# Shares of attention transposed by VectorE and ScalarE in place of TensorE, from group 10 on

## Chip, core and metric

The kernel runs on one core of one Trainium2 chip. The metric is the device time of one execution in microseconds. The engines go by the names of the profile: PE is TensorE, DVE is VectorE, ACT is ScalarE, POOL is GpSimd, SP issues the DMAs. Each engine works through its own queue of instructions in order.

## What is computed

Windowed attention over 8 batches of 8 heads, 576 positions and 64 columns a head, in fp32, and behind it a channel-mixing block with a one-step time shift. Cut to what matters:

```python
scores = scale * np.matmul(q, k.transpose(0, 1, 3, 2))
mask = (rel >= 0) & (rel < 64)                 # rel = query position - key position
attn = softmax(where(mask, scores, -1e9))      # shares
x = np.matmul(attn, v)                         # heads side by side: 8 x 576 x 512

x_prev = x shifted by one position
xk = mu_k * x + (1 - mu_k) * x_prev
xr = mu_r * x + (1 - mu_r) * x_prev
k = np.maximum(xk @ w_k, 0)                    # 512 -> 1024
v = k * k @ w_v                                # 1024 -> 512
r = 1 / (1 + np.exp(-(xr @ w_r)))              # 512 -> 512
out = r * v
```

The weights arrive as 64-bit floats and are turned to fp32 on the chip.

## The kernel before

**Blocks and groups.** The 576 positions of a batch are 9 blocks of 64. Two consecutive blocks of the 72 form a group (36 groups, `GROUPS`). A query block meets at most its own and the previous block of keys, so a group needs 2 x 64 query rows of all heads. A group's scores fill one bank of PSUM, as 128 partitions (two halves of 64 query rows) by 8 pairs of head and block, by 128 keys.

**Attention of a group** (`soften`, line 464). VectorE folds the 128 keys of each row into 64 (`pack`: each row's window takes exactly 64 of them), takes the maximum (`most`), subtracts it (`less`); ScalarE takes the exponential (`exp`); VectorE sums (`total`), inverts the sums (`shares`) and multiplies (`scale`), so that the tile `pr` (128 x 512) holds the shares. In the groups of `LEAN` the subtraction, the exponential and the sum are eight ScalarE instructions instead (`exps`), one for each of the 8 pairs, with the maximum as bias and an accumulated sum. The value products need the shares with the keys on the partitions. That transposition is `flip` (line 516): four TensorE transposes of 128x128 into the PSUM tile `t`. VectorE then writes them to SBUF twice, multiplied by two masks (`keep`, line 521), as the tile `pt`: keys of the own block and keys of the previous block. The value products (`values`, 48 or 64 small matmuls) read `pt` and write the PSUM tile `x`, which ScalarE copies to `xu` (`keep_x`).

**Bursts.** `burst` (line 391) issues the scores of group t and the values of group t-1 together on TensorE; in the first groups they are issued apart.

**Units.** The channel mixing runs over units of 4, 5 and then nine times 7 blocks (448 columns). In each unit the blended inputs `xk` and `xr` are split into a rounded part and a rest (`high` on ScalarE, `low` on VectorE), as are the weights and the squares `ks`, and each product is three matmuls per chunk instead of one in full fp32. Eight `k` products take 12 matmuls each, four `r` products 12, four `v` products 24: 240 matmuls a unit. In the first unit the products are plain fp32. ScalarE empties the banks of k and r (three activations per k product, four per r product), VectorE those of v; the results are stored by SP. Three PSUM banks (`m`) are shared by all products.

**The order of the work** comes from a planner in the program. Each `Piece` (line 103) has an engine, a key, an assumed cost, the pieces it needs and the buffers (`Hold`) that it takes and uses. `play` (line 117) walks through an assumed time: an engine that is free takes the ready piece of lowest key. A piece is ready when each piece it needs on another engine has been done for a `lag` (160 ns if not given otherwise), for TensorE pieces of key 60 or more for another 1500 ns (`SLACK`, `STEADY`), and when its buffers are free. The order found is each engine's order on the chip. The keys of the attention groups stand in `BEGIN` (line 42), those of the decoding of the 28 weight chunks in `DECODE`, of their splitting in `SPLIT`, of the first two units' blends in `MIX_0` and `MIX_1`; unit u has keys from 40 u on. `ORDER` (line 54) is the order in which SP issues the first loads (`w` is the next weight chunk, `k0` the keys of group 0).

Of the kernel before, what the change touches and what calls it, by code (L numbers as in the profile page):

```python
# [10 lines left out]
F32 = mybir.dt.float32  # L11
# [7 lines left out]
P = 128  # L19
# [16 lines left out]
TB = 6  # L36
# [2 lines left out]

STEP = 6  # L40
USTEPS = 40
BEGIN = (-81.5, -50.0, -17.0, -17.0, -3.5, 20.0, 21.0, 55.5, 61.0, 70.0, 70.5, 79.5, 93.5, 113, 123, 133, 143,
    153, 163, 173, 183, 196, 210, 223, 236, 250, 263, 277, 286, 295, 304, 312, 322, 332, 342, 352)
DECODE = (0.0, -63.5, -41.0, -15.5, -38.5, -58.0, -19.5, -38.5, -43.0, -28.5, -43.0, -34.5, 45.5, 53.5, 33.5,
    38.0, 46.0, 75.5, 36.5, 48.0, 11.0, 32.0, 34.5, 61.0, 31.0, 41.0, 79.5, 57.5)
MIX_0 = (-78.0, -17.5, -25.5, 6.0)
MIX_1 = (-59.5, -87.5, 44.5, 59.0)
SPLIT = (36.5, 8.5, 54.5, 56.0, 41.5, 47.0, 58.5, 18.5, 55.5, 155.0, 60.0, 133.0, 98.5, 82.0, 77.0, 111.0,
    104.5, 69.5, 168.0, 137.0, 172.5, 109.5, 143.5, 44.0, 125.0, 94.0, 130.5, -3.5)
PE_LOW = set()  # L50
LEAN = {0, 1, 2, 3, 4, 5, 8, 10, 11}
SPARE = {512: 1, 256: 2}
LOADED = 6
ORDER = (*"w w w k0 v2 w q0 v0 w w v1 k1 q1 w w w w q2 w w v3 w w w w k3 w k2 w v5 w k5 w w k4 w q4".split(),
         *"q3 w w w w q5 v4 w w".split())
LINK = 160
SLACK = 1500
STEADY = 60
# [7 lines left out]
def attn_rwkv_kernel(ctx, tc, qT, kT, v2, mu_k, mu_r, w_k, w_v, w_r, out):  # L66
# [3 lines left out]
    at = ctx.enter_context(tc.tile_pool(name="at", bufs=2))  # L70
    act = ctx.enter_context(tc.tile_pool(name="act", bufs=1))
    tmp = ctx.enter_context(tc.tile_pool(name="tmp", bufs=2))
# [5 lines left out]
    class Engine:  # L78
# [5 lines left out]
        def __getattr__(self, name):  # L84
# [1 line left out]
            return lambda *args, **kw: tc.keep_in_program_order(op(*args, **kw))  # L86

    pe, dve, sca, pool, dma = (Engine(e) for e in (nc.tensor, nc.vector, nc.scalar, nc.gpsimd, nc.sync))
    room = {"tmp": TB, "m": 3, "s": 1, "t": 1, "x": 1, "pr": 2, "sums": 4, "pt": 2, "xu": 2,
            **{f"w{wc}": count for wc, count in SPARE.items()}, "ks": 8, "r": R_BUFS, "xr": 1, "xk": 1, "q": 2, "k": 2, "v": 3}  # L90

    def slow(key):
        return SLACK if key >= STEADY else 0
# [103 lines left out]
    for j in range(2):  # L197
        rows = slice(j * W, (j + 1) * W)
# [43 lines left out]
    def decode(n, loaded):  # L242
        ws, _, i, c, wc = chunks[n]
        key = DECODE[n]
        word = Hold("tmp")
# [27 lines left out]
    def split(n):  # L273

        ws, _, i, c, wc = chunks[n]
        key = SPLIT[n]
        ps, bank = [], Hold("m")
# [80 lines left out]
    def block(g, s):  # L358
        return divmod(2 * g + s, NB)

    banks, weights, sums, flipped, sided, crossed = {}, {}, {}, {}, {}, {}
    xs_of, got, opened_x = {}, {}, {}
    chain = {}

# [26 lines left out]
    def burst(key, gs, gv):  # L391
# [31 lines left out]
        if gs is not None:  # L423
            soften(key, gs, p, takes[0])
# [36 lines left out]
    def wide(tile_, count):  # L461
        return tile_.unsqueeze(1).to_broadcast([P, count, W])

    def soften(key, g, p, bank):
        rows, sm = Hold("pr"), Hold("sums")

        lean = g in LEAN
        both = block(g, 0)[1] and block(g, 1)[1]

        def pack():  # L470
            s4 = banks[g]
            weights[g] = at.tile([P, 8, W], F32, name="pr", bufs=2)
            sums[g] = [at.tile([P, 8], F32, name=nm, bufs=4) for nm in ("most", "sums", "rs")]
            if both:
                s8 = s4.rearrange("q h e k -> q (h e) k")
                dve.copy_predicated(s8[:, :, :W], wide(own.bitcast(U32), 8), s8[:, :, W:])
                return
            for s in range(2):
                for h in range(2):
                    e = s4[:, h, 2 * s:2 * s + 2]  # L480
                    if block(g, s)[1]:
                        dve.copy_predicated(e[:, :, :W], wide(own.bitcast(U32), 2), e[:, :, W:])
                    else:
                        dve.tensor_add(e[:, :, :W], e[:, :, W:], wide(hide, 2))

        def most():
            s8 = banks[g].rearrange("q h e k -> q (h e) k")
            dve.tensor_reduce(sums[g][0], s8[:, :, :W], axis=AX.X, op=ALU.max)
            if lean:
                dve.tensor_scalar_mul(sums[g][0], sums[g][0], -SCALE)  # L490

        def less():
            s8 = banks[g].rearrange("q h e k -> q (h e) k")
            dve.tensor_sub(weights[g], s8[:, :, :W], sums[g][0].unsqueeze(2).to_broadcast([P, 8, W]))

        def exp():
            sca.activation(weights[g], weights[g], AF.Exp, scale=SCALE)

        def exps():
            s8 = banks[g].rearrange("q h e k -> q (h e) k")  # L500
            for e in range(8):
                sca.activation(weights[g][:, e], s8[:, e, :W], AF.Exp, scale=SCALE, bias=sums[g][0][:, e:e + 1],
                               accum_out=sums[g][1][:, e:e + 1])

        def total():
            dve.tensor_reduce(sums[g][1], weights[g], axis=AX.X, op=ALU.add)

        def shares():
            _, total, rs = sums[g]
            dve.tensor_scalar_add(rs, total, EPS)  # L510
            dve.reciprocal(rs, rs)

        def scale():
            dve.tensor_mul(weights[g], weights[g], sums[g][2].unsqueeze(2).to_broadcast([P, 8, W]))

        def flip():
            ps = flipped[g] = ps_t.tile([P, 4, P], F32, name="t")
            for e in range(4):
                pe.transpose(ps[:, e], weights[g][:, 2 * e:2 * e + 2].rearrange("q e k -> q (e k)"), ident)

        def keep(a):
            if a == 1:
                sided[g] = at.tile([P, 2, 4, P], F32, name="pt", bufs=2)
            dve.tensor_mul(sided[g][:, a].rearrange("q e (j r) -> q (e j) r", j=2),
                           flipped[g].rearrange("q e (j r) -> q (e j) r", j=2), wide(sides[:, a], 8))

        tbank, kept = Hold("t"), Hold("pt")
        q = Piece("DVE", key + 0.5, 610 if both else 960, pack, [p], [rows, sm], [bank])
        q = Piece("DVE", key + 0.5, 610 + 80 * lean, most, [q], uses=[bank])
        if lean:  # L530
            q = Piece("ACT", key + 0.5, 8 * 290, exps, [q], uses=[bank])
        else:
            q = Piece("DVE", key + 0.5, 610, less, [q], uses=[bank])
            q = Piece("ACT", key + 0.5, 540, exp, [q])
            q = Piece("DVE", key + 0.5, 610, total, [q])
        q = Piece("DVE", key + 0.5, 300, shares, [q])
        q = Piece("DVE", key + 0.5, 610, scale, [q], uses=[sm], port=True)
        q = Piece("PE", key + 1, 430, flip, [q], [tbank], [rows], lag=300, kind="t", slack=slow(key))
        q = Piece("DVE", key + 1, 610, lambda: keep(1), [q], [kept], [tbank])
        chain["kept", g] = Piece("DVE", key + 1, 610, lambda: keep(0), [q], uses=[tbank])  # L540
        chain["pt", g] = kept

    def prefetch(t):
        for what, g in (("q", t + 2), ("k", t + 2), ("v", t + 2)):
            if LOADED <= g < GROUPS:
                load(what, g, key=BEGIN[t])

# [198 lines left out]
    arrived["mu"] = Piece("POOL", -98, 250, opposite, [p], port=True)  # L746
    for what in ORDER:
        if what == "w":
# [4 lines left out]
    for t in range(GROUPS + 1):  # L753
        key = BEGIN[t] if t < GROUPS else BEGIN[-1] + 9
        if 1 <= t <= 2:
# [7 lines left out]
    for u, nb in enumerate(UNITS):  # L763
        n = nb * W
        base = u * USTEPS
        gate, k2 = [], []
        xk, xr = ([], Hold("xk"), []), ([], Hold("xr"), [])
        if u == 0:
            keys = MIX_0
        elif u == 1:  # L770
            keys = MIX_1
        else:
# [46 lines left out]
```

## Time and profile before

| | |
|---|---|
| median of 3 runs | 639.86 us (638.74 to 640.3) |
| the profiled execution | 639.49 us |
| its span, first to last instruction | 637.8 us |
| TensorE busy | 606.7 us, 95% |
| VectorE busy | 434.8 us, 68% |
| ScalarE busy | 350.3 us, 55% |
| granted TensorE clock | 1.0 |
| flips: matmuls `t<-ident,pr` | 144, of 0.28 us each, busy 22.5 us |

The busy time of an engine is the union of its instructions' times. Matmuls overlap one another, so that their durations sum to more than they hold the queue. Nearly all rows carry one line, L86, since a helper records every operation; they are told apart by tile: `m<-xk,w` and `m<-xr,w` are k and r products, `m<-ks,w` v products, `s` scores, `t` flips, `x` values, `pr` shares, `pt` masked shares. The idle time in a row stands ahead of its instructions, with what ended it.

### The profile page before, as it was taken

The numbers are of one execution on the slowest core, as the hardware profiler recorded it, in microseconds if no ns is written. First come the engines' busy times: TensorE is split into PE (matmuls) and PEld (weight loads), VectorE is DVE, ScalarE is ACT, GpSimd is POOL, SyncE is SP. The second block draws the span as 40 slices with busy tenths as digits, with TensorE's granted clock in tenths as the row PEclk, the third lists the DMA queues.
The fourth block names the chain that finished last, engine by engine and source line by source line (L and its number), as shares of the span: only waits on it lengthen the run. The fifth ranks groups of instructions, "written<-read, shape, count | busy, mean of one in ns | idle before, by whom it ended". The sixth has DMA issues, their size and how long they took to land.

```text
span 637.8 us, 14586 instructions
## 1 busy us (share of the span) xinstructions
PE 606.7 (95%) x6032; PEld 553.2 (87%) x6032; DVE 434.8 (68%) x923; ACT 350.3 (55%) x809; POOL 4.4 (1%) x27
## 2 busy tenths in 40 slices
PE   0389999999999999999999999999999999999997
PEld 0268899999999999999999999999999999999996
DVE  6899998964696696669358745965795596254211
ACT  2768789467626643663474366346525652662650
POOL 2000000000000000000000000000000000000000
PEclk9999999999999999999999999999999999999999
DMA  8982241231243223322222310241232211001001
GB/s 262 365 296 59 77 133 51 81 99 52 61 120 98 61 69 98 88 59 72 74 60 74 102 51 14 80 141 32 72 117 74 59 33 44 1 1 59 0 1 58
DMA packets 77409, 53.37 MB, mean 84 GB/s; under 512 B 12832, under 2 KB 73760, under 8 KB 77344
## 3 DMA queue, kind: packets, MB, share of 16 engines
q1 hardware_dynamic: 77056, 52.45, 27.2%
q8 instruction: 47, 0.77, 0.5%
q14 instruction: 18, 0.15, 0.1%
q10 hardware_dynamic: 288, 0.00, 0.0%
HBM read 43.00 MB, written 9.44 MB: 82 GB/s over the span
## 4 chain that ended last, share of the span: by engine, by line
PE 87%; DVE 7%; DMA 4%; SPq 1%; issue 0%
PE m L86 76%; PE s L86 5%; PE x L86 4%; DMA w<-w_k 2%; PE t L86 2%; DVE w L86 2%; DVE wt L86 2%; DMA k<-kT 1%; SPq L86 1%; DMA w<-w_v 1%; DVE most L86 0%; DVE pt L86 0%; DVE s L86 0%; DVE r L86 0%; DVE pr L86 0%
## 5 line engine op out<-in xcount | busy, mean ns | idle before, releaser
L86 PE MATMUL m<-xk,w 128*128 128x448 f32 (+2 forms) x1024 | 219.6, 363 | 0.0
L86 PE MATMUL m<-ks,w 128*128 128x448 f32 (+2 forms) x1024 | 216.6, 362 | 0.4 <-DVE r L86 0.4
L86 PEld LDWEIGHTS m<-ks,w 128*128 128x128 f32 x1024 | 187.0, 188 | 15.2 <-DVE r L86 0.8
L86 PEld LDWEIGHTS m<-xk,w 128*128 128x128 f32 x1024 | 186.7, 188 | 14.9 <-ACT kf L86 0.4
L86 PE MATMUL m<-xr,w 128*128 128x448 f32 (+2 forms) x512 | 114.0, 368 | 1.0 <-DVE xr L86 1.0
L86 DVE TENSOR_TENSOR ks<-kf,ks 128x448 fp32r<-128x448 f32 (+1 forms) x80 | 48.7, 610 | 96.4 <-ACT ks L86 96.1
L86 PEld LDWEIGHTS m<-xr,w 128*128 128x128 f32 x512 | 94.8, 191 | 9.9 <-DVE xr L86 2.1
L86 ACT ACTIVATE kf<-m 128x448 f32<-128x448 f32 (+2 forms) x88 | 45.7, 522 | 84.9 <-PE m L86 83.0
L86 PE MATMUL s<-k,q 64*64 64x128 f32 (+1 forms) x1152 | 40.5, 281 | 20.6 <-DMA q<-qT 11.8
L86 ACT CAST xk<-e 128x448 fp32r<-128x448 f32 (+1 forms) x40 | 22.4, 560 | 68.4 <-DVE e L86 68.4
L86 PEld LDWEIGHTS s<-k,q 64*64 64x64 f32 x1152 | 31.8, 140 | 30.8 <-DMA q<-qT 11.8
L86 DVE TENSOR_TENSOR pt<-t,sides 128x512 f32<-128x512 f32 x72 | 48.3, 685 | 10.9 <-PE t L86 10.9
L86 DVE SCALAR_TENSOR_TENSOR r<-th,r 128x448 f32<-128x448 f32 (+2 forms) x44 | 26.1, 593 | 37.0 <-ACT r L86 37.0
L86 ACT ACTIVATE kf<-kf 128x448 f32<-128x448 f32 (+1 forms) x80 | 45.3, 567 | 2.2
L86 ACT CAST ks<-kf 128x448 fp32r<-128x448 f32 (+1 forms) x80 | 44.3, 556 | 2.3
L86 PE MATMUL x<-pt,v 64*64 64x64 f32 x2176 | 40.0, 223 | 3.8 <-DVE pt L86 3.8
L86 PEld LDWEIGHTS x<-pt,v 64*64 64x64 f32 x2176 | 38.1, 139 | 5.1 <-issue 2.8
L86 DVE SCALAR_TENSOR_TENSOR r<-m,r 128x448 f32<-128x448 f32 (+2 forms) x44 | 25.9, 590 | 23.5 <-PE m L86 23.3
L86 ACT COPY xu<-x 128x512 f32<-128x512 f32 (+1 forms) x44 | 22.2, 513 | 28.7 <-PE x L86 28.4
L86 ACT ACTIVATE th<-m 128x448 f32<-128x448 f32 (+2 forms) x44 | 23.4, 531 | 23.7 <-PE m L86 23.5
L86 DVE COPY_PREDICATED s<-own,s 128x512 f32<-128x512 uint32 (+1 forms) x44 | 24.1, 547 | 8.7 <-PE s L86 8.3
L86 ACT CAST xr<-e 128x448 fp32r<-128x448 f32 (+1 forms) x40 | 22.4, 560 | 12.7 <-DVE e L86 12.3
(51 smaller groups left out, 520.7 us busy)
## 6 DMA issues: line engine op xcount, KB each, us to landing
k<-kT SPq DMA_DIRECT2D x28, 384.0 KB, 3.7
v<-v SPq DMA_DIRECT2D x128, 64.0 KB, 2.5
q<-qT SPq DMA_DIRECT2D x32, 256.0 KB, 3.1
w<-w_k SPq DMA_DIRECT2D x8, 512.0 KB, 6.6
w<-w_v SPq DMA_DIRECT2D x16, 256.0 KB, 6.2
outT<-r SPq DMA_DIRECT2D x12, 224.0 KB, 1.9
w<-w_r SPq DMA_DIRECT2D x4, 512.0 KB, 4.6
k<-kT SPq DMA_DIRECT2D x8, 256.0 KB, 3.2
```

The source lines that it names most:

```text
L86: return lambda *args, **kw: tc.keep_in_program_order(op(*args, **kw))
```

## The change

Groups 0 to 9 are flipped as before. From group 10 on (`PE_FLIPS`), the shares are transposed without TensorE. `turn` has VectorE transpose each square of 32x32 within its place, over the whole 128x512 tile, twice: once into `tr` and once into `fl`. The squares on the diagonal of each 128x128 matrix are then right in `fl`. `move` has ScalarE copy the other twelve squares of each matrix from `tr` to their places in `fl`: 12 copies, each from one quarter of the partitions to another, 32 partitions by 4 x 32 elements. `keep` then reads `fl` from SBUF instead of `t` from PSUM. `tr` and `fl` have one buffer each; `pt` has one instead of two. In the planner, `turn` is a VectorE piece of 1220 ns and `move` a ScalarE piece of 12 x 190 ns. Groups 7 and 9 join `LEAN`. The keys and the order of the first loads are other numbers; from group 21 on the keys of the groups are the same.

```diff
-BEGIN = (-81.5, -50.0, -17.0, -17.0, -3.5, 20.0, 21.0, 55.5, 61.0, 70.0, 70.5, 79.5, 93.5, 113, 123, 133, 143,
-    153, 163, 173, 183, 196, 210, 223, 236, 250, 263, 277, 286, 295, 304, 312, 322, 332, 342, 352)
+BEGIN = (-114.0, -48.0, -13.0, -10.0, 10.5, 14.0, 19.5, 36.0, 41.5, 72.5, 77.5, 78.0, 83.0, 121.5, 128.5,
+    132.0, 134.5, 147.5, 172.0, 176.5, 187.0, 196, 210, 223, 236, 250, 263, 277, 286, 295, 304, 312, 322, 332,
+    342, 352)
...
-LEAN = {0, 1, 2, 3, 4, 5, 8, 10, 11}
+LEAN = {0, 1, 2, 3, 4, 5, 7, 8, 9, 10, 11}
...
-ORDER = (*"w w w k0 v2 w q0 v0 w w v1 k1 q1 w w w w q2 w w v3 w w w w k3 w k2 w v5 w k5 w w k4 w q4".split(),
-         *"q3 w w w w q5 v4 w w".split())
+PE_FLIPS = 10
+ORDER = (*"w w k0 w w q0 v2 w w v0 k1 q1 w v1 w w w v3 w w q2 w w w w v5 w w w w k2 q3 w k4 w w k3 w".split(),
+         *"w w q4 v4 w q5 k5 w".split())
...
-            ... "t": 1, "x": 1, "pr": 2, "sums": 4, "pt": 2, "xu": 2,
+            ... "t": 1, "tr": 1, "fl": 1, "x": 1, "pr": 2, "sums": 4, "pt": 1, "xu": 2,
...
+        def turn():
+            for name in ("tr", "fl"):
+                turned[g, name] = at.tile([P, 4, P], F32, name=name, bufs=1)
+                dve.transpose(turned[g, name].rearrange("k e (b q) -> k (e b) q", b=4),
+                              weights[g].rearrange("q e (b k) -> q (e b) k", b=2))
+            flipped[g] = turned[g, "fl"]
+
+        def move():
+            for b in range(4):
+                for x in range(4):
+                    if b != x:
+                        sca.copy(flipped[g][x * 32:(x + 1) * 32, :, b * 32:(b + 1) * 32],
+                                 turned[g, "tr"][b * 32:(b + 1) * 32, :, x * 32:(x + 1) * 32])
...
-        q = Piece("PE", key + 1, 430, flip, [q], [tbank], [rows], lag=300, kind="t", slack=slow(key))
-        q = Piece("DVE", key + 1, 610, lambda: keep(1), [q], [kept], [tbank])
-        chain["kept", g] = Piece("DVE", key + 1, 610, lambda: keep(0), [q], uses=[tbank])
+        source = [tbank]
+        if g < PE_FLIPS:
+            q = Piece("PE", key + 1, 430, flip, [q], source, [rows], lag=300, kind="t", slack=slow(key))
+        else:
+            source, moved = [Hold("fl")], Hold("tr")
+            q = Piece("DVE", key + 0.5, 1220, turn, [q], [*source, moved], [rows])
+            q = Piece("ACT", key + 0.5, 12 * 190, move, [q], (), [moved])
+        q = Piece("DVE", key + 1, 610, lambda: keep(1), [q], [kept], source)
+        chain["kept", g] = Piece("DVE", key + 1, 610, lambda: keep(0), [q], uses=source)
```

More of the change, by code (lines that the diff above doesn't have):

```diff
@@ L41 @@
 USTEPS = 40
-BEGIN = (-81.5, -50.0, -17.0, -17.0, -3.5, 20.0, 21.0, 55.5, 61.0, 70.0, 70.5, 79.5, 93.5, 113, 123, 133, 143,
-    153, 163, 173, 183, 196, 210, 223, 236, 250, 263, 277, 286, 295, 304, 312, 322, 332, 342, 352)
[L44 to L49, printed above, removed]
+BEGIN = (-114.0, -48.0, -13.0, -10.0, 10.5, 14.0, 19.5, 36.0, 41.5, 72.5, 77.5, 78.0, 83.0, 121.5, 128.5,
+    132.0, 134.5, 147.5, 172.0, 176.5, 187.0, 196, 210, 223, 236, 250, 263, 277, 286, 295, 304, 312, 322, 332,
+    342, 352)
+DECODE = (-37.5, -76.5, -39.5, -29.5, -36.0, -79.5, -29.5, -45.0, -74.5, -34.5, -21.5, -35.5, 31.5, 28.5,
+    33.5, 26.5, 28.5, 77.0, 39.5, 25.0, -8.0, -15.5, 40.0, 92.5, 11.0, 36.5, 56.0, 47.5)
+MIX_0 = (-52.0, -13.5, -50.0, -22.5)
+MIX_1 = (-76.0, -98.5, 34.0, 15.0)
+SPLIT = (25.5, 24.0, 40.0, 56.5, 4.5, -23.0, 50.0, 9.0, 62.5, 170.0, 82.5, 154.5, 100.5, 116.0, 100.5, 136.0,
+    131.5, 90.5, 202.0, 161.0, 176.5, 149.0, 166.0, 54.5, 130.5, 104.5, 136.5, 17.0)
 PE_LOW = set()
-LEAN = {0, 1, 2, 3, 4, 5, 8, 10, 11}
+LEAN = {0, 1, 2, 3, 4, 5, 7, 8, 9, 10, 11}
 SPARE = {512: 1, 256: 2}
 LOADED = 6
-ORDER = (*"w w w k0 v2 w q0 v0 w w v1 k1 q1 w w w w q2 w w v3 w w w w k3 w k2 w v5 w k5 w w k4 w q4".split(),
-         *"q3 w w w w q5 v4 w w".split())
+PE_FLIPS = 10
+ORDER = (*"w w k0 w w q0 v2 w w v0 k1 q1 w v1 w w w v3 w w q2 w w w w v5 w w w w k2 q3 w k4 w w k3 w".split(),
+         *"w w q4 v4 w q5 k5 w".split())
 LINK = 160
@@ L88, in attn_rwkv_kernel @@
     pe, dve, sca, pool, dma = (Engine(e) for e in (nc.tensor, nc.vector, nc.scalar, nc.gpsimd, nc.sync))
-    room = {"tmp": TB, "m": 3, "s": 1, "t": 1, "x": 1, "pr": 2, "sums": 4, "pt": 2, "xu": 2,
+    room = {"tmp": TB, "m": 3, "s": 1, "t": 1, "tr": 1, "fl": 1, "x": 1, "pr": 2, "sums": 4, "pt": 1, "xu": 2,
             **{f"w{wc}": count for wc, count in SPARE.items()}, "ks": 8, "r": R_BUFS, "xr": 1, "xk": 1, "q": 2, "k": 2, "v": 3}
@@ L359, in block @@
         return divmod(2 * g + s, NB)
-    banks, weights, sums, flipped, sided, crossed = {}, {}, {}, {}, {}, {}
+    banks, weights, sums, flipped, turned, sided, crossed = {}, {}, {}, {}, {}, {}, {}
     xs_of, got, opened_x = {}, {}, {}
@@ L522, in keep @@
             if a == 1:
-                sided[g] = at.tile([P, 2, 4, P], F32, name="pt", bufs=2)
+                sided[g] = at.tile([P, 2, 4, P], F32, name="pt", bufs=1)
             dve.tensor_mul(sided[g][:, a].rearrange("q e (j r) -> q (e j) r", j=2),
                            flipped[g].rearrange("q e (j r) -> q (e j) r", j=2), wide(sides[:, a], 8))
+        def turn():
[10 more added lines that the diff above has]
+                                 turned[g, "tr"][b * 32:(b + 1) * 32, :, x * 32:(x + 1) * 32])
         tbank, kept = Hold("t"), Hold("pt")
```

## The prediction

> **What bounds the kernel now.** I read the page first, then busy time by stage, then the chain of waits. The page's first two parts:
>
> ```profile
> span 637.8 us, 14586 instructions
> PE 606.7 (95%) x6032; PEld 553.2 (87%) x6032; DVE 434.8 (68%) x923; ACT 350.3 (55%) x809; POOL 4.4 (1%) x27
> ...
> PE   0389999999999999999999999999999999999997
> ...
> PEclk9999999999999999999999999999999999999999
> ```
>
> TensorE is busy in every slice but the first three and the last, at the full granted clock. A busy average doesn't say that it sets the end, so I cut the span where the stages change (start-up, the first ten groups, groups 10 to 35, the rest of the products):
>
> ```profile
> core 0: us, PE busy (x) PEld busy (x) DVE busy (x) ACT busy (x) POOL busy (x), PEclk, DMA share, GB/s
> 0.00:40.00 40.00, 13.39 (x221) 10.63 (x222) 32.15 (x71) 19.21 (x57) 3.69 (x20) 1.00 0.94 312
> 40.00:150.00 110.00, 109.14 (x1254) 99.78 (x1253) 98.03 (x242) 83.46 (x266) 0.33 (x3) 1.00 0.33 98
> 150.00:540.00 390.00, 390.00 (x4098) 355.81 (x4097) 273.13 (x560) 201.13 (x400) 0.42 (x4) 1.00 0.25 72
> 540.00:638.00 98.00, 94.16 (x466) 86.96 (x464) 31.45 (x52) 46.50 (x88) 0.00 (x0) 1.00 0.06 19
> ```
>
> Between 150 and 540 us TensorE has no idle time; VectorE works 273 of 390 us (70%), ScalarE 201 (52%). The first 40 us are loads and decoding. The chain, read along one group late in the run, shows what a flip takes of TensorE, and its first and last rows here are those of groups 10 and 35:
>
> ```profile
> 150.03 0.44 PE t L86 x4
> ...
> 353.82 9.30 PE m L86 x45
> 363.12 0.44 PE t L86 x4
> 363.56 10.33 PE m L86 x51
> 373.88 1.03 PE s L86 x32
> ...
> 533.53 0.44 PE t L86 x4
> ```
>
> The four transposes hold the queue for 0.44 us. The products behind them keep their pace (10.33 us / 51 = 0.2026 us each; the 45 ahead of them take 9.30 - 45 x 0.2026 = 0.18 us more, which is the turn from the value products, not from the flip). So 0.44 us is the whole slot: nothing is hidden in its neighbours.
>
> **The change part by part.**
>
> *Removed: 26 flips on TensorE (groups 10 to 35).* 26 x 0.44 = 11.44 us, all in the stretch where TensorE never idles.
>
> *Added on VectorE: two transposes of 128x512 per group.* No row shows one. The nearest rows, and the pace of two instructions of that size back to back:
>
> ```profile
> L86 DVE TENSOR_TENSOR pr<-pr,rs 128x512 f32<-128x512 f32 x36 | 24.8, 689 | 0.7
> L86 DVE TENSOR_SCALAR wt<-wt 128x512 uint32<-128x512 uint32 x12 | 5.0, 422 | 0.1
> ...
> 339.98 0.69 DVE L86 TENSOR_TENSOR pr<-s,most 128x512 f32<-128x512 f32 x1
> 340.59 0.62 DVE L86 TENSOR_TENSOR d<-xu 128x448 f32<-128x448 f32 x1
> ```
>
> Bounds for the two: 2 x 0.42 = 0.84 us to 2 x 0.69 = 1.38 us. I take the pace of the 512-element row, 340.59 - 339.98 = 0.61, so 1.22 us, since most rows of this size lie there; the planner assumes the same 1.22. Over 26 groups 31.7 us: VectorE goes to 304.8 of about 378.6 us, 81%.
>
> *Added on ScalarE: 12 copies of 32 partitions x 128 elements per group.* None is in the trace either. The nearest rows by size:
>
> ```profile
> L86 ACT COPY xu<-x 128x256 f32<-128x256 f32 x16 | 5.7, 374 | 7.1 <-PE x L86 7.0
> L86 ACT COPY xu<-xu 128x4 f32<-128x4 f32 x9 | 1.8, 200 | 0.6
> ...
> 35.09 0.20 ACT L86 COPY xu<-xu 128x4 f32<-128x4 f32 x1
> 35.20 0.50 ACT L86 ACTIVATE e<-xu,mu 128x256 f32<-128x256 f32 x1
> ...
> 332.79 0.58 ACT L86 ACTIVATE th<-th 128x448 f32<-128x448 f32 x1
> 333.26 0.57 ACT L86 ACTIVATE r<-r 128x448 f32<-128x448 f32 x1
> ```
>
> From SBUF the next instruction follows after 0.11 us at 4 elements and 0.47 us at 448, so by the straight line 0.21 us at 128; 12 x 0.21 = 2.5 us, against 2.28 in the plan. Bounds: 12 x 0.11 = 1.3 us below, 12 x 0.374 = 4.5 us above (the longer copy's whole duration, with no overlap). I take 2.5 us, since the copies are independent like the two rows used. Over 26 groups 65 us: ScalarE goes to 266 of 378.6 us, 70%.
>
> The Trainium skill, "VectorE: DVE Perf Modes", section "The TRN2 errata — SBUF-src ops pay a fixed extra latency per instruction", has a ScalarE copy from SBUF cost 224 cycles at 1.2 GHz beside one per element, paid again by each small tile, which speaks against cutting one move into twelve: 12 x 352 cycles = 3.5 us by that estimate. By it ScalarE would be busy 91 us more instead of 65, and 1.2 us behind plan in each group. The trace agrees on the duration (200 ns at 4 elements), but the next instruction started after 0.11 us, so its overlap decides here.
>
> *The path of a group gets longer.* The tightest group of the run is the last:
>
> ```profile
> 531.36 0.68 DVE L86 TENSOR_TENSOR pr<-pr,rs 128x512 f32<-128x512 f32 x1
> ...
> 533.37 0.60 PE L86 MATMUL t<-ident,pr 128*128 128x128 f32 x4
> ...
> 534.01 0.69 DVE L86 TENSOR_TENSOR pt<-t,sides 128x512 f32<-128x512 f32 x1
> ...
> 535.16 0.68 DVE L86 TENSOR_TENSOR pt<-t,sides 128x512 f32<-128x512 f32 x1
> ...
> 538.16 1.16 PE L86 MATMUL x<-pt,v 64*64 64x64 f32 x64
> ```
>
> From scaled shares (532.04) to the first masked product (534.01) it is 1.97 us now, and 1.22 + 2.5 = 3.7 us with hand-overs after: 1.75 us more. The masked shares would be ready at 537.6 instead of 535.84, still ahead of 538.16. The code explains the gap: behind key 60 a TensorE piece is planned 160 + 1500 ns after what it needs. That 1.66 us covers a plan that is too short by as much; without it, each microsecond of lateness would be 26 us. What is queued behind the new waits: on ScalarE the rectify, square and round instructions of the k products; on VectorE the rest terms and gates. TensorE waits for both.
>
> The slack that ScalarE has, and what else stands in its queue:
>
> ```profile
> L86 ACT ACTIVATE kf<-m 128x448 f32<-128x448 f32 x72 | 39.2, 545 | 83.1 <-PE m L86 81.9
> ...
> L86 ACT COPY xu<-x 128x512 f32<-128x512 f32 x28 | 16.6, 592 | 21.7 <-PE x L86 21.5
> ...
> L86 ACT ACTIVATE pr<-pr 128x512 f32<-128x512 f32 x27 | 17.0, 630 | 15.7 <-DVE pr L86 15.6
> ```
>
> It idles 83 us in front of the first of these, waiting for TensorE. There are three product banks; one k or r product is 12 x 0.2026 = 2.43 us, so an eviction may start 2 x 2.43 - 0.55 = 4.3 us late before TensorE notices. One move fits (2.5 us).
>
> *Costed at nothing:* one buffer for the masked shares (values of group t-1 are issued in the same TensorE burst as the scores of group t, so they are read long before group t's shares are ready; cover gone, one value burst's 1 us); the eight per-head exponentials in groups 7 and 9 (two VectorE passes of 0.61 us less, more on ScalarE, at a time when TensorE is busy 109 of 110 us); the moved prefetches on SP behind 40 us (DMA share 0.25). POOL's queue gets nothing.
>
> *The start, planned anew.* SP now issues q0 ahead of v2 (timeline of SP and TensorE, and the row of the transfers of v):
>
> ```profile
> 2.66 3.46 SPq L86 DMA_DIRECT2D v<-v  x4
> 6.16 0.59 SPq L86 DMA_DIRECT2D w<-w_r  x1
> 6.79 0.43 SPq L86 DMA_DIRECT2D q<-qT  x1
> ...
> 11.84 1.56 PE L86 MATMUL s<-k,q 64*64 64x64 f32 x32 [11.84 <-DMA q<-qT]
> ...
> 38.08 2.93 PE L86 MATMUL m<-xr,w 128*128 128x256 f32 x6 [0.51 <-DVE xr L86]
> ...
> v<-v SPq DMA_DIRECT2D x128, 64.0 KB, 2.5
> ```
>
> v2 is four transfers of 64 KB, 256 KB; at the 312 GB/s of the first 40 us it takes 0.8 us of the wire, so the first scores can come that much sooner (q0's issue, 3.46 us sooner, isn't the limit at a DMA share of 0.94). Whether it reaches the first product at 38.08 hangs on VectorE, which decodes at the same time (32 of 40 us busy). Bounds: -0.8 us, and +2 us if the new order of decodes delays a group by three of their steps (3 x 0.69). I take -0.5 us. For stray waits of TensorE behind 150 us, of which it has none now, I add 0.5.
>
> *Sum.* The profiled execution took 639.49 us (span 637.8 and 1.7 around it); the median of the runs is 639.86. 639.49 - 11.44 - 0.5 + 0.5 = **628.0 us**.
>
> **The rivals.**
>
> *ScalarE gives half back.* Where the r products run (48 of a unit's 240 matmuls, one fifth), ScalarE has four activations of about 0.47 us per 2.43 us product. There a move at its upper bound (4.5 us), behind the exponential and the x copy (0.6 us each), makes an eviction 5.7 us late: 1.4 us of stall. A fifth of 26 groups is five: 7 us, time 635. For it: banks have no planned margin like the 1.5 us. Against it: the copies' likely pace, under half of that bound.
>
> *The detour is too slow, and the kernel slower.* The place is the value burst at the head of TensorE's queue. If transposes run at half my pace (2.44 us) and copies without overlap at 0.30 us (3.6 us), the pair takes 6.04 us where the plan has 3.50: 2.54 late, 0.88 beyond the 1.66 margin, 26 times: +22.9, time 651. It decides against the change from 1.66 + (11.44 + 1.9)/26 = 2.17 us of lateness on. For it: neither instruction has a row. Against it: both prices must be wrong together. The Trainium skill, "VectorE: DVE Perf Modes", section "Rules for kernel authors", has the same preference: TensorE for a 128x128 transpose if PSUM will do. No run here shows it yet.
>
> *The start gains more.* If group 1, whose k and q are also issued sooner, pulls the first product in by 4 us: 639.5 - 11.4 - 4 = 624.
>
> *The slots are gone, but the start or VectorE's 81% takes all of it.* A start later by 5 us and the ScalarE loss of 7 together: 640, no change.
>
> **How the numbers follow.** The forecast 0.66, with its own range 625 to 631 (the start's -0.8 to +2, up to 1.5 us of waits, 0.3% between runs). Half given back 0.14; more gained at the start 0.06; no change 0.06; slower 0.08. The range 623.5 to 636.5 takes in the second and third and leaves out about 0.2. A measurement of this kernel can tell 0.3%, 1.9 us: faster 0.66 + 0.14 + 0.06 = 0.86, same 0.06, slower 0.08.
>
> **What would show it.** In the changed profile: 40 flip matmuls instead of 144; TensorE busy about 11 us less and still without idle time behind 45 us; transposes near 0.69 us and a pair's pace of 1.22; copies starting every 0.2 us, a set of 12 in about 2.5; VectorE near 81% and ScalarE near 70% in the long stretch; the first product at 36 to 40 us. Wrong would be: idle time of TensorE ahead of the value products released by the masked shares (the detour), or ahead of m products released by ScalarE (the banks), of more than 3 us in all.

## The result, and the profile after

The changed kernel takes **659.22 us** (658.18 to 660.71), the kernel before on the same chip 639.36 us. The ratio is **1.031, with a 95% interval of 1.0298 to 1.0323**: 3% slower, where 628.0 us (623.5 to 636.5) was forecast. The profiled execution took 660.71 us.

The page of the changed kernel: the span, the busy times, TensorE's slices and its granted clock, and the shares of the chain of waits; behind them the chain's shares in the kernel before.

```profile
span 658.4 us, 14782 instructions
PE 605.3 (92%) x5928; PEld 545.1 (83%) x5928; DVE 461.9 (70%) x973; ACT 440.9 (67%) x1151; POOL 3.9 (1%) x27
...
PE   0489999998899899989999998999999998999997
...
PEclk9999999999999899989999999999999999999999
...
PE 42%; DVE 25%; ACT 24%; DMA 5%; issue 2%; SPq 0%; ACTq 0%
```

```profile
PE 87%; DVE 7%; DMA 4%; SPq 1%; issue 0%
```

The 104 flip matmuls are gone (6032 to 5928), as meant. But TensorE now has slices that aren't full, two of them at a lower clock, and the chain, in which it had 87% before, runs for half of the span through VectorE and ScalarE. The stretches of the prediction, cut the same way (columns as there):

```profile
0.00:40.00 40.00, 12.76 (x219) 10.28 (x220) 32.79 (x73) 20.32 (x60) 3.14 (x20) 1.00 0.94 311
40.00:150.00 110.00, 109.96 (x1259) 100.91 (x1258) 95.70 (x239) 87.30 (x299) 0.32 (x3) 1.00 0.34 99
150.00:540.00 390.00, 370.52 (x3684) 332.18 (x3683) 281.49 (x568) 275.40 (x673) 0.42 (x4) 0.99 0.24 70
540.00:658.00 118.00, 112.02 (x771) 101.75 (x769) 51.87 (x95) 57.90 (x121) 0.00 (x0) 0.98 0.07 24
```

Between 150 and 540 us TensorE had no idle time before; now it has 390.00 - 370.52 = 19.5 us. ScalarE went from 201 to 275 us of that stretch. Who waits for whom in the whole run (us in total, times, the longest): first TensorE's waits ahead of products, then VectorE's wait for the squares that it needs for the masked shares.

```profile
PE m L88 <- ACT kf L88: 14.1, 12, 2.0
...
PE m L88 <- ACT r L88: 7.5, 4, 2.5
...
PE m L88 <- DVE r L88: 0.3, 1, 0.3
...
DVE pt L88 <- ACT fl L88: 63.0, 26, 3.8
```

TensorE waits 21.6 us for evictions by ScalarE (14.1 for k products, 7.5 for r products), 18.9 of them in the long stretch, and nowhere in that stretch for masked shares. The new instructions, by groups:

```profile
L88 ACT COPY fl<-tr 32x128 f32<-32x128 f32 x312 | 92.4, 296 | 31.2 <-DVE fl L88 27.7
L88 DVE STREAM_TRANSPOSE tr<-pr 128x512 f32<-128x512 f32 x26 | 18.3, 706 | 0.3
L88 DVE STREAM_TRANSPOSE fl<-pr 128x512 f32<-128x512 f32 x26 | 17.4, 669 | 0.0
```

312 copies are busy 92.4 us: 0.296 us each, with no overlap. One group in time order shows what that does:

```profile
281.85 0.57 ACT L88 ACTIVATE r<-r 128x448 f32<-128x448 f32 x1
281.88 0.70 DVE L88 STREAM_TRANSPOSE tr<-pr 128x512 f32<-128x512 f32 x1
282.51 0.67 DVE L88 STREAM_TRANSPOSE fl<-pr 128x512 f32<-128x512 f32 x1
283.11 0.58 DVE L88 SCALAR_TENSOR_TENSOR r<-th,r 128x448 f32<-128x448 f32 x1
283.22 3.67 ACT L88 COPY fl<-tr 32x128 f32<-32x128 f32 x12 [0.80 <-DVE fl L88]
286.92 0.54 ACT L88 ACTIVATE th<-m 128x448 f32<-128x448 f32 x1
286.92 1.29 DVE L88 TENSOR_TENSOR pt<-fl,sides 128x512 f32<-128x512 f32 x2 [3.24 <-ACT fl L88]
287.36 0.54 ACT L88 ACTIVATE r<-m 128x448 f32<-128x448 f32 x1
...
287.95 0.75 PE L88 MATMUL m<-ks,w 128*128 128x448 f32 x2 [2.48 <-ACT r L88]
```

The two transposes take 283.11 - 281.88 = 1.23 us. The twelve copies take 3.67 us, to the next start 3.70: 0.308 us each. ScalarE had waited 0.80 us for them, so between 282.42 and 286.92 it empties no bank. TensorE runs out of banks and stands still for 2.48 us, until the second activation on `m` at 287.36 has ended.

### The profile page after: what moved, and what is told of

It is laid out like the page before. It is cut to its first block, busy times and chain, and to the rows that moved or that the text cites. A ratio compares the mean times of both kernels' runs of the same rounds, so it can differ in the third digit from the quotient of the medians.

```text
span 658.4 us, 14782 instructions
## 1 busy us (share of the span) xinstructions
PE 605.3 (92%) x5928; PEld 545.1 (83%) x5928; DVE 461.9 (70%) x973; ACT 440.9 (67%) x1151; POOL 3.9 (1%) x27
## 4 chain that ended last, share of the span: by engine, by line
PE 42%; DVE 25%; ACT 24%; DMA 5%; issue 2%; SPq 0%; ACTq 0%
PE m L88 36%; ACT fl L88 12%; ACT kf L88 5%; DVE e L88 3%; DVE pr L88 3%; PE s L88 3%; PE x L88 2%; ACT ks L88 2%; DVE r L88 2%; DMA w<-w_k 2%; DVE tr L88 2%; ACT r L88 2%; DVE sums L88 2%; DVE fl L88 2%; DVE xr L88 2%
## 5 line engine op out<-in xcount | busy, mean ns | idle before, releaser
L88 PE MATMUL m<-xr,w 128*128 128x448 f32 (+2 forms) x512 | 116.7, 373 | 9.3 <-ACT kf L88 6.0
L88 PEld LDWEIGHTS m<-xr,w 128*128 128x128 f32 x512 | 96.1, 194 | 20.9 <-ACT kf L88 7.8
L88 ACT COPY fl<-tr 32x128 f32<-32x128 f32 x312 | 92.4, 296 | 31.2 <-DVE fl L88 27.7
L88 DVE TENSOR_TENSOR pt<-fl,sides 128x512 f32<-128x512 f32 x52 | 34.5, 688 | 63.0 <-ACT fl L88 63.0
L88 PE MATMUL s<-k,q 64*64 64x128 f32 (+1 forms) x1152 | 40.5, 281 | 20.6 <-DMA q<-qT 11.5
L88 ACT ACTIVATE pr<-s,most 128x64 f32<-128x64 f32 x88 | 26.2, 324 | 6.6 <-DVE most L88 6.3
```

## The experiments

The runs stand here by the question that each answers. "Path" is the way of a group's shares from the scores to `pt`; "load" is what ScalarE has to do, wherever it stands.

| kernel | time, us | ratio to before, 95% | TensorE idle, 150 to 540 us | mean spacing of score bursts, groups 10 to 35 |
|---|---|---|---|---|
| before | 639.4 | | 0 | 15.26 |
| after | 659.22 | 1.0298 to 1.0323 | 19.5 | 16.95 |
| keys alone | 637.15 | 0.9959 to 0.998 | 0 | 15.33 |
| 8 of 12 copies | 633.12 | 0.9886 to 0.9922 | 3.5 | 15.92 |
| 7 of 12 copies | 629.07 | 0.9822 to 0.9855 | 0.8 | 15.77 |
| true price in the planner | 651.14 | 1.0172 to 1.0204 | 14.3 | 16.95 |
| all 12 on GpSimd | 645.35 (one execution) | | 11.6 | 16.75 |
| 6 on ScalarE, 6 on GpSimd | 630.21 | 0.9839 to 0.9869 | 1.0 | 15.72 |
| the same, and 6 copies beside the path | 636.15 | 0.9937 to 0.997 | 5.9 | 15.97 |
| 3 on ScalarE, 9 on GpSimd | 640.46 | 1.0002 to 1.0027 | 8.8 | 16.46 |
| true price, other keys | 647.66 | 1.0102 to 1.0142 | 11.3 | 16.85 |
| true price, from group 22 on | 635.47 | 0.9908 to 0.9943 | 1.7 | 16.30 |

Idle is 390 less TensorE's busy time in that stretch; the spacing is the time from the first scores of group 10 to those of group 35, by 25. The kernels with 7 or 8 copies leave out some of the squares; they show time alone.

### Keys and start alone

```diff
-PE_FLIPS = 10
+PE_FLIPS = 36
```

> The changed kernel with all 36 groups flipped by TensorE: the new keys, the new order of loads, LEAN and the single pt buffer alone. Theory C (the new keys are at fault): 650 or more. Theories A and B (the move is at fault): within 3 us of the kernel before, 636 to 642, with no idle time of TensorE behind 150 us.

637.15 us: the new keys, orders, `LEAN` and the single `pt` buffer are together worth 2.1 us (1.3 to 2.6) and leave TensorE without idle time. The loss lies in the detour.

### Fewer copies, the order unchanged

```diff
-                    if b != x:
+                    if b != x and b ^ x != 3:
```

> Leaves out 4 of the 12 copies of each move (the squares exchanged between quarters 0 and 3, and 1 and 2), so those squares of the shares keep a wrong content; the order of all other work is that of the changed kernel. In the changed kernel a move took 3.67 us (286.92 - 283.22 and its like), 0.306 us a copy, where the plan has 2.28. Theory A (the order was written for a move of 2.28 us, and TensorE's waits for banks are the 1.39 us that each move is late): 8 x 0.306 = 2.45 us is nearly what the plan has, so TensorE idles under 4 us behind 150 us and the time is 626 to 632. Theory B (ScalarE has too much to do in that stretch, whatever the order): a third of the added work is gone and a third of the 31 us lost against the forecast, 648. Theory C (the new keys are at fault): no change, 655 to 661.

With the same order of work, 8 copies give 633.12 us, 26 us less than 12 (1.1 us above the range of theory A, and far from the other two). Eight copies at 0.308 us take 2.48 us, 0.20 more than the 2.28 planned. One copy fewer takes out that rest (7 x 0.308 = 2.16):

```diff
-                    if b != x:
+                    if b != x and b ^ x != 3 and (b, x) != (0, 1):
```

> As the run with eight copies, but with seven (five squares of the shares keep a wrong content): 7 x 0.308 = 2.16 us, 0.12 us less than the plan has, where eight took 2.48, 0.20 more, and twelve 3.70, 1.42 more. Theory A (no margin: TensorE waits for what a move is late): the 6 us that eight copies still lost go, 625 to 628. Theory B (it is the amount of work on ScalarE): one copy in twelve less gives 2.6 us of the 31, 630 to 632.

629.07 us, and 0.8 us of idle time. The time lies between the two expected ranges; that the idle time is gone speaks for theory A. So a detour that keeps its planned 2.28 us does bring a gain of 8.1 us over the keys alone, out of the 11.44 of the slots. The transposes, VectorE's share and the single buffer can cost at most the 3.3 us that are left; the loss comes of what the copies take.

### Why a copy takes 0.308 us

```diff
-                        sca.copy(flipped[g][x * 32:(x + 1) * 32, :, b * 32:(b + 1) * 32],
-                                 turned[g, "tr"][b * 32:(b + 1) * 32, :, x * 32:(x + 1) * 32])
+                    if g < 16:
+                        copy(x, b, b, x)          # quarter to, column to, quarter from, column from
+                    elif g < 21:
+                        copy(b, x, x, b)          # the source changes each time
+                    elif g < 26:
+                        copy(b, b, b, x)          # no crossing, same place written three times
+                    elif g < 31:
+                        copy(1, b, 0, x)          # always quarter 0 to quarter 1
+                    else:
+                        copy(None, b, None, x)    # 128 partitions
```

> The changed kernel with the 12 copies of a move in five forms, by group, 32x128 elements each unless said (from group 21 on the shares come out wrong): 10 to 15 as they are (three copies from one quarter of the partitions, each to another); 16 to 20 the loops swapped (three to one quarter, each from another); 21 to 25 from and to the same quarter, which changes every three copies; 26 to 30 all from quarter 0 to quarter 1; 31 to 35 all 128 partitions. What a copy takes to the next one's start was 0.306 us. Theory A1 (a change of the quarter that is written or read makes a copy wait for the one before): 0.20 to 0.22 us where nothing changes (26 to 30, and 31 to 35), and two of three in 21 to 25; 0.306 in 10 to 20. Theory A2 (a copy of SBUF never overlaps the next): 0.30 in all five. Theory A3 (crossing from one quarter to another is what costs): 0.20 to 0.22 in 21 to 25 and 31 to 35 alone.

Sets of twelve in the timeline of ScalarE: as in the change, with source and destination swapped, always from quarter 0 to quarter 1, and of 128 partitions.

```profile
215.93 3.68 ACT L88 COPY fl<-tr 32x128 f32<-32x128 f32 x12 [0.95 <-DVE fl L88]
...
253.41 3.68 ACT L88 COPY fl<-tr 32x128 f32<-32x128 f32 x12 [1.83 <-DVE fl L88]
...
418.21 3.54 ACT L88 COPY fl<-tr 32x128 f32<-32x128 f32 x12 [2.65 <-DVE fl L88]
...
502.42 3.54 ACT L88 COPY fl<-tr 128x128 f32<-128x128 f32 x12 [0.33 <-DVE fl L88]
```

Swapping changes nothing, but the sums hide two effects. From start to start, the last two sets go 0.33, 0.33 and then 0.205 us, over and over: a copy that writes the same place again costs 0.33, the others 0.205, crossing or not. In the sets without crossing (groups 21 to 25) the third is 0.31; there the quarter changes. A second kernel of forms writes another place each time and changes one thing at a time:

```diff
+                    elif g < 18:
+                        to, frm = b, b            # no crossing, quarter changes after three
+                    elif g < 22:
+                        to, frm = 1, 0            # always 0 to 1
+                    elif g < 26:
+                        to, frm = 1 + n % 2, 0    # only the destination changes
+                    elif g < 30:
+                        to, frm = 0, 1 + n % 2    # only the source changes
+                    else:
+                        to, frm = None, None      # 128 partitions; from group 33 on the same place
```

> The 12 copies of a move once more in several forms by group, now with another block of columns written each time (from group 14 on the shares come out wrong): 10 to 13 as they are; 14 to 17 from and to the same quarter of the partitions, which changes every three copies; 18 to 21 all from quarter 0 to quarter 1; 22 to 25 from quarter 0 to 1 and 2 in turn; 26 to 29 from 1 and 2 in turn to quarter 0; 30 to 32 all 128 partitions; 33 to 35 all 128 partitions, the same block of columns written each time. In the run with five forms a copy started 0.205 us after one of the same quarters that wrote another place, 0.31 after a change of quarters, and 0.33 after one that wrote the same place. If that is the rule: 0.31 in 10 to 13, 22 to 25 and 26 to 29; 0.205 in two of three and 0.31 in the third in 14 to 17; 0.205 in 18 to 21 and 30 to 32; 0.33 in 33 to 35. If crossing from a quarter to another counted by itself, 18 to 21 would show 0.3 as well.

Groups 14, 18, 22, 26, 30 and 33, in this order:

```profile
214.14 2.81 ACT L88 COPY fl<-tr 32x128 f32<-32x128 f32 x12 [0.95 <-DVE fl L88]
...
277.78 2.50 ACT L88 COPY fl<-tr 32x128 f32<-32x128 f32 x12 [0.79 <-DVE fl L88]
...
341.39 3.84 ACT L88 COPY fl<-tr 32x128 f32<-32x128 f32 x12
...
407.06 3.84 ACT L88 COPY fl<-tr 32x128 f32<-32x128 f32 x12 [2.64 <-DVE fl L88]
...
479.06 2.50 ACT L88 COPY fl<-tr 128x128 f32<-128x128 f32 x12 [0.70 <-DVE fl L88]
...
522.31 3.94 ACT L88 COPY fl<-tr 128x128 f32<-128x128 f32 x12 [2.65 <-DVE fl L88]
```

Always from quarter 0 to quarter 1, twelve copies take 2.50 us, as twelve of 128 partitions do: about 0.20 us from start to start, the 0.21 of the prediction. Crossing costs nothing here. As soon as the source's or the destination's quarter is another than in the copy before, it is 0.31 to 0.32; three changes among twelve give 2.81. In the change every copy has another pair of quarters, and at 0.308 us from start to start each begins only when its predecessor (0.296 us) has ended. The Trainium skill, "VectorE: DVE Perf Modes", section "Two Vector instructions with no wait between them", tells such a hold for VectorE: an instruction that starts in another quadrant waits until all earlier ones have finished. These rows show the like of ScalarE.

### The true price in the planner

```diff
-            q = Piece("ACT", key + 0.5, 12 * 190, move, [q], (), [moved])
+            q = Piece("ACT", key + 0.5, 12 * 306, move, [q], (), [moved])
```

> The changed kernel with the planner told the measured price, 12 x 306 ns a move, all keys as they are. Theory A (price mis-sized): the order now fits, VectorE's wait for the move and TensorE's waits for banks shrink, but the keys were chosen for the shorter move: 638 to 650. Theory B (too much work on ScalarE, whatever the order): no change, 655 to 661.

651.14 us: an order that knows the price gets back 8 us, and 12 remain against before. The price itself, not only the order written for a lower one, is too high. Nor is it these keys alone: with the true price and other keys for groups 7 to 35 (`LEAN` without 10) it was 647.66.

```diff
-    ... 19.5, 36.0, 41.5, 72.5, 77.5, 78.0, 83.0, 121.5, 128.5, 132.0, 134.5, 147.5, 172.0, 176.5, 187.0, ...
+    ... 19.5, 33.0, 37.5, 42.0, 75.5, 78.5, 89.0, 100.5, 101.5, 123.0, 133.0, 156.5, 158.0, 159.0, 164.5, ...
...
+            q = Piece("ACT", key + 0.5, 12 * 306, move, [q], (), [moved])
```

> The changed kernel with the planner told the true price (12 x 306 ns) and other keys for groups 7 to 35, sought for that price; group 10 leaves LEAN. If the 651 of the order with the true price came of keys that were chosen for a shorter move, 630 to 640. If it comes of the move itself (ScalarE's work and the path of a group), 643 to 651.

### Load on ScalarE, or length of the path

All copies on GpSimd take the load off ScalarE, and leave the path long:

```diff
-                        sca.copy(flipped[g]...
+                        pool.tensor_copy(flipped[g]...
...
+            q = Piece("POOL", key + 0.5, 12 * 300, move, [q], (), [moved])
```

> The 12 copies of a move on GpSimd, planned at 12 x 300 ns; ScalarE gets none. GpSimd's price for such a copy is not known. Theory A (ScalarE's work ahead of the bank evictions is what TensorE waits for): TensorE's waits for kf and r go; with up to 0.35 us a copy the time is 628 to 645, and what is lost stands ahead of the value products (pt late). Theory B (the longer path of a group by itself costs): 650 or more with waits ahead of the value products even at 0.3 us a copy. At 0.5 us a copy or more both give over 650 by the path.

```profile
313.75 4.76 POOL L88 COPY fl<-tr 32x128 f32<-32x128 f32 x12 [12.53 <-DVE fl L88]
```

Twelve copies take 4.76 us there, 0.40 each, and the time is 645.35 us: still slower than before, with ScalarE at 193 of 390 us, less than it had before the change. Without any load on ScalarE the longer path costs 645.35 - 637.15 = 8.2 us against the keys alone, though a part of that can come of the order, which was written for 3.6 us a move. The waits are not where either theory had them: 8.6 us stand ahead of k products, for their blended inputs, and 0.4 us ahead of value products. Six copies on each engine, side by side, shorten it:

```diff
+ON_ACT = 6
...
+        def move(engine, first, last):
+            squares = [(b, x) for b in range(4) for x in range(4) if b != x]
+            for b, x in squares[first:last]:
+                (sca.copy if engine == "ACT" else pool.tensor_copy)(...)
...
+            q, p = (Piece(e, key + 0.5, cost * (last - first), ..., [q], (), [moved])
+                    for e, cost, first, last in (("ACT", 306, 0, ON_ACT), ("POOL", 395, ON_ACT, 12)))
+        q = Piece("DVE", key + 1, 610, lambda: keep(1), [q, p], [kept], source)
```

> The whole computation: each move shared, six copies on ScalarE (planned at 306 ns each, as measured) and six on GpSimd (planned at 395 ns each, from the run with all on GpSimd: 4.71 us / 12 = 0.39), side by side; all keys of the changed kernel. Theory A (the order loses just as much as a move is longer than planned): ScalarE's part takes 1.85 us and GpSimd's 2.4, the order is written for just that, so TensorE idles under 3 us behind 150 us and the time is 625 to 630, faster than both. Theory B (VectorE's two transposes or the longer path of a group cost by themselves): 633 or more.

```profile
span 628.3 us, 14827 instructions
PE 595.8 (95%) x5928; PEld 541.4 (86%) x5928; DVE 464.0 (74%) x973; ACT 398.1 (63%) x995; POOL 61.5 (10%) x183
...
PE 72%; DVE 15%; DMA 5%; ACT 4%; SPq 1%; issue 1%; POOL 0%; ACTq 0%; DVEq 0%; POOLq 0%
```

**630.21 us**, ratio 0.9854 (0.9839 to 0.9869): the whole computation, 1.5% faster than the kernel before and 0.2 us above the expected 625 to 630. TensorE has 1.0 us of idle time in the long stretch. From here, load and path were varied. First the load: six more copies on ScalarE, into the share tile that isn't read any more, so that no one waits for what they write. (The planner keeps the tiles `tr` and `pr` taken until these copies are through; what that costs wasn't separated.)

```diff
+        def aside():
+            waste = weights[g].rearrange("q (e b) k -> q e (b k)", b=2)
+            for b, x in squares[6:]:
+                sca.copy(waste[...], turned[g, "tr"][...])
...
+            Piece("ACT", key + 0.5, 6 * 306, aside, [t], (), [moved, rows])
```

> The whole computation: as the run with six copies on ScalarE and six on GpSimd, and ScalarE then makes the other six copies as well, into the used-up shares, where nobody reads them. ScalarE has the changed kernel's 12 copies of 0.308 us, and the order knows it, but the masked shares wait for six of them (1.85 us) and for GpSimd (2.4 us) alone. Theory L (ScalarE's added work is what the true price costs): 645 to 655, like the 651 of the order with the true price. Theory P (the path of a group is what it costs: the bursts of a group come at 16.95 us from one another in that run and in the changed kernel, 15.3 where TensorE flips): 628 to 634, with bursts under 16 us apart.

Then the path, with less on ScalarE:

```diff
+ON_ACT = 3
```

> The whole computation: three copies of each move on ScalarE (0.92 us) and nine on GpSimd (3.55 us at 395 ns, as planned). ScalarE has a quarter of the changed kernel's added work, but the masked shares wait for 3.55 us of copies, close to its 3.70. Theory L (ScalarE's added work): 628 to 633. Theory P (the path of a group): 638 to 648, with bursts 16.3 us apart or more.

The first scores of group 10 and of group 35, in the timelines of TensorE, before:

```profile
140.75 1.10 PE L86 MATMUL s<-k,q 64*64 64x128 f32 x32
...
522.20 1.10 PE L86 MATMUL s<-k,q 64*64 64x128 f32 x32
```

after:

```profile
137.94 1.10 PE L88 MATMUL s<-k,q 64*64 64x128 f32 x32
...
561.74 1.10 PE L88 MATMUL s<-k,q 64*64 64x128 f32 x32
```

with six more copies beside the path:

```profile
136.55 1.10 PE L89 MATMUL s<-k,q 64*64 64x128 f32 x32
...
535.89 1.10 PE L89 MATMUL s<-k,q 64*64 64x128 f32 x32
```

and with 3 copies on ScalarE and 9 on GpSimd:

```profile
136.71 1.10 PE L89 MATMUL s<-k,q 64*64 64x128 f32 x32
...
548.25 1.10 PE L89 MATMUL s<-k,q 64*64 64x128 f32 x32
```

The load costs 636.15 - 630.21 = 5.9 us, a time between the ranges of the two theories; the path 640.46 - 630.21 = 10.2 us, within the range of theory P (its profiled execution has one stretch at half the clock, an estimated 1.7 us of it); both at once (true price, all on ScalarE) 651.14 - 630.21 = 20.9. The two together make 16.1; 4.8 come on top when both meet.

How a longer path costs time is in the spacing. A group's share of a unit is 240 x 0.2026 / 3.5 = 13.9 us of products; with scores (1.03), values and the turn (0.18) TensorE needs about 16.0 us per group when it does no flips. The values' price is in the chain of the kernel before:

```profile
374.92 0.93 PE x L86 x64
```

A new burst can't start before the path of the one ahead is through, since it holds that group's value products. In the timelines, from a group's first scores to the end of its masked shares it was 12.1 us before and 15.5 after (means of groups 10 to 34); the next burst came 3.2 us behind that before, and 1.5 after.

While the spacing is under 16.0 us, attention runs ahead of the products and builds up a lead; above it, the lead is used up, and then TensorE lacks inputs. Before, the spacing was 15.26, after 16.95: (16.95 - 16.0) x 25 = 24 us, against 20.9 lost with the same spacing at the true price. With 3 and 9 it is 16.46: 11.5 us, against 10.2. These two agreements are weak evidence: the spacing contains TensorE's idle time, and the changed kernel, with the same 16.95, loses 29.0 us (659.22 - 630.21). What tells more is what TensorE waits for. In the run with 3 and 9 it is the blended inputs of the k products, which need the values, and no longer evictions in the first place:

```profile
PE m L89 <- DVE xk L89: 3.2, 3, 1.2
...
PE m L89 <- ACT xk L89: 2.5, 3, 1.1
```

At the true price with all twelve on ScalarE, evictions still come first (8.8 of the 14.3 us in the long stretch, against 0.7 for blended inputs), so for that kernel the used-up lead isn't shown by its waits.

If the lead counts, the same copies at the full price must cost little where a lead is already there. The last run has TensorE flip up to group 21 and the detour only behind it:

```diff
-PE_FLIPS = 10
+PE_FLIPS = 22
...
+            q = Piece("ACT", key + 0.5, 12 * 306, move, [q], (), [moved])
```

> The planner told the true price (12 x 306 ns), and the move only from group 22 on: TensorE flips 22 groups, 14 are moved. Theory P (a group's path sets the pace once the lead of the attention groups is used up): with 14 long paths and the lead that 22 short ones leave, TensorE waits little: 632 to 638. Theory L (each move costs TensorE what ScalarE does ahead of an eviction, whatever the lead): 14/26 of the 14 us between 651 and the 637 without any move: 644 to 646.

635.47 us. 14 of the 26 expensive moves are still there. Had each cost the same, they would give 14/26 of the 20.9 us, 11 us, and a time over 640; there are 1.7 us of idle time instead. The first scores of groups 10, 22 and 35:

```profile
137.81 1.10 PE L88 MATMUL s<-k,q 64*64 64x128 f32 x32
...
316.66 0.90 PE L88 MATMUL s<-k,q 64*64 64x128 f32 x32
...
545.28 1.10 PE L88 MATMUL s<-k,q 64*64 64x128 f32 x32
```

Up to group 22 the bursts come every 14.90 us, where TensorE needs 16.47 with flips (16.03 + 0.44): a lead of about 18.8 us by this estimate. Behind it they come every 17.59 us, where TensorE needs 16.03 without flips, and use about 20.3 us of lead, with the 1.7 us of idle time. A fixed price per move is rejected; a lead that is built up and spent fits.

## Why the prediction was wrong, point by point

**The slots on TensorE (26 x 0.44 = 11.44 us): nearly right.** With 7 copies 8.1 us of them are kept, with 6 and 6 6.9 (637.15 - 630.21). The rest was not followed further.

**The two transposes (1.22 us): right.** 1.23 us in the timeline, 0.706 and 0.669 us each.

**The copies (12 x 0.21 = 2.5 us): the step that failed.** The prediction says "I take 2.5 us, since the copies are independent like the two rows used". They measured 0.308, 3.70 us a move. Independent data was not what mattered: the two rows used both began in the first quarter, and the copies never stay in the same pair of quarters. 3.70 lay inside the bounds of 1.3 to 4.5. The prediction's paragraph on the Trainium skill, "VectorE: DVE Perf Modes", section "The TRN2 errata — SBUF-src ops pay a fixed extra latency per instruction", had the other end: by its estimate 352 cycles are 0.293 us, measured 0.296, and 91 us more on ScalarE and 3.5 us per move met 92.4 us of copies and 3.67. The step from there, that the "overlap decides here", is what was wrong: there was none.

**The path ("1.75 us more. The masked shares would be ready at 537.6 instead of 535.84, still ahead of 538.16"): right on the place it looked at, wrong on what it is for.** From the first transpose to the first masked product, 286.92 - 281.88 = 5.04 us in the group shown, where 1.22 + 2.5 = 3.72 were expected. The margin of 1.66 us ahead of the value burst held even so: TensorE's waits have none for masked shares in the long stretch (with the true price in the planner they have 2.1 us there, in two places). But the length of the path also sets how soon the next burst comes, and that was not priced at all: 1.7 us more spacing (16.95 against 15.26), where 16.47 (16.03 + 0.44) was TensorE's own limit before and 16.0 is now.

**"One move fits (2.5 us)" of 4.3 us: failed with the price, and on its own count.** The 4.3 took one eviction of 0.55 us to free a bank. An r product's bank is read by two activations (286.92 and 287.36, TensorE goes on at 287.95, 1.03 us in all), so that only 2 x 2.43 - 1.03 = 3.8 us are to be had there. ScalarE was away for 0.80 + 3.70 = 4.5 us. The waiting of ScalarE for the transposes, in its own queue, was not counted either.

**The start (-0.5, bounds -0.8 to +2): outside its bounds.** The keys alone, all of them and not the start's only, brought 2.1 us.

**VectorE at 81%, ScalarE at 70%.** 72% and 71% in the long stretch, but of a run in which both waited longer. VectorE was busy 27.1 us more (31.7 expected, less the passes of `LEAN`).

**Stray waits (+0.5): 21.9 us.** They make the result, with two things that no term held. Each stop drains the pipeline: a matmul lasts 0.37 us and the next follows after 0.2026, so 17 stops cost about 2.9 us beside their idle time, by this estimate. And behind the three longest the clock fell, two of them in these rows:

```profile
219.82 4.26 PE L88 MATMUL m<-xr,w 128*128 128x448 f32 x12 [1.96 <-ACT kf L88]
...
557.55 4.26 PE L88 MATMUL m<-xk,w 128*128 128x448 f32 x12 [2.00 <-ACT kf L88]
```

Twelve matmuls in 4.26 us, where 12 x 0.2026 + 0.17 = 2.60 is their pace: 1.66 us lost each, 5.0 in three. From the 7-copy kernel: 629.07 + (21.9 - 0.8) + 2.9 + 5.0 = 658.1, of 659.22 measured.

**The rivals.** "ScalarE gives half back" had the right place, the evictions behind a move, and the right reason, banks without a planned margin. It was limited to the r products; 14.1 of the 21.6 us were at k products, and the time was 659, not 635. "The detour is too slow" had the copies at 0.30 us and called slower, but put the loss at the value burst, where there was none, and wanted both prices wrong. One was enough: its 2.17 us of lateness from which the change loses was never reached (3.70 - 2.28 = 1.42). The sign that the prediction named for its failure, idle time ahead of m products released by ScalarE of over 3 us, is what came.

**What stays open.** How the 8 us between the order for 2.28 us and that for 3.67 divide: the profiled executions differ by 9.5 us of span, 5.7 of them idle time of TensorE and 3.7 its busy time, and the second has no stop with half the clock behind it, but drain and clock weren't separated; the 4.8 us by which load and path together cost more than each alone; and the 3 to 5 us of the slots that no variant kept. It is open, too, how much of the loss at the true price is the used-up lead and how much the evictions.

## What to carry to other kernels

Price a moved operation by a row of the same kind with the same neighbours: whether consecutive copies change partitions between them made 0.308 us out of 0.205 here, and one run of the bare operation would have told. Before work is taken off the bound engine, check whether what replaces it lies on a path that sets the spacing of later work; idle time of the engine that takes it over says nothing on that. If the replacement is small pieces, share them between two engines that are free, as the 6 and 6 here, and give the planner the measured prices.

## What the runs showed of the hardware

- **ScalarE's copies overlapped only where the quarters of the partitions stayed the same.** fp32 copies of 32x128 from SBUF to SBUF: 0.20 us from start to start with source and destination quarters as before, 0.31 to 0.32 when one changes, 0.33 when the same place is written again. Crossing from quarter 0 to quarter 1 cost nothing in itself.
- **A GpSimd copy of that size took 0.40 us in a row**, 4.76 for twelve. Beside six on ScalarE, six took 3.19 us once, 0.53 each, in the timelines of the 6 and 6 kernel:

```profile
288.07 1.83 ACT L89 COPY fl<-tr 32x128 f32<-32x128 f32 x6 [3.77 <-DVE fl L89]
...
288.14 3.19 POOL L89 COPY fl<-tr 32x128 f32<-32x128 f32 x6 [13.63 <-DVE fl L89]
```

- **Stops of 2 us can halve TensorE's clock.** In the changed kernel idle times of 1.96, 2.48 and 2.00 us were each followed by 3.41 us at half the clock; one of 1.85 and shorter ones were not. The length of a single stop doesn't decide it: in the second kernel of forms one of 1.85 us was followed by half the clock and one of 2.12 us was not, and in the kernel with 3 and 9 two stops of 0.80 and 0.86 us, with one recorded matmul between them, were. Two of the changed kernel's stretches (columns as above, the clock is the 0.50):

```profile
220.20:223.50 3.30, 3.30 (x11) 2.95 (x10) 1.49 (x3) 3.28 (x9) 0.00 (x0) 0.50 0.02 5
288.50:291.80 3.30, 3.30 (x10) 2.96 (x9) 1.25 (x2) 3.28 (x8) 0.00 (x0) 0.50 0.00 0
```

The Trainium skill, "TensorE: Matmul & The Clock Gate", section "Part 1: The HAM clock gate (the "warmup" mystery)", puts the drop behind an idle window of about 3.4 us. The length at half clock agrees (3.41 us); the single stops that brought it on were shorter here.
